# Moving weight splits, gate quotients and query products in a polysketch-attention and expert-mix kernel, with one more expert's block in three passes

## The chip, the cores and the metric

The kernel runs on one core of a Trainium2 chip, in one launch. The metric is the device time in microseconds (us): lower is better. All times below are of runs on the chip.

## The reference

The first half is a polynomial-sketch attention on q, k and v of shape (4, 4, 1088, 32), the second half a mix of four expert networks on the 4352 tokens that come out of it (all in float32):

```python
def phi(x):                       # S1, S2: 8 x 32
    a = einsum('rd,bhsd->bhsr', S1, x); b = einsum('rd,bhsd->bhsr', S2, x)
    return einsum('bhsi,bhsj->bhsij', a, b).reshape(..., 64)
kv, z = einsum('bhsf,bhsd->bhfd', phi(k), v), phi(k).sum(axis=2)
attn = einsum('bhsf,bhfd->bhsd', phi(q), kv) / (einsum('bhsf,bhf->bhs', phi(q), z) + 1e-6)
x = attn.transpose(0, 2, 1, 3).reshape(4352, 128)
p = domain_probs / (domain_probs.sum(-1) + 1e-9)          # 4352 x 4
out = sum over e of p[:, e] * (relu(x @ w1[e]) @ w2[e])     # w1[e]: 128 x 1024, w2[e]: 1024 x 128
```

## The kernel before

**Tiling.** The 4352 tokens go through the experts in 11 chunks: chunk 0 and chunk 10 have 128 tokens, chunks 2 and 3 have 480, the others 448. A chunk takes 16 steps, four for each expert, and a step has two half steps, one for each block of 128 hidden columns (8 blocks for an expert). A half step is called h here, counted over the whole kernel from 0: chunk 1 has h = 32 to 63, chunk 2 has 64 to 95, and so on. The attention of the later batches is cut into units (128, 448 and 512 tokens in the first batch, 576 and 512 in the others), and its pieces are laid between the half steps by lists of half steps.

**First product.** In chunks 1 to 9 a block's hidden values come from three passes of matmuls in the reduced type fp32r, with the tokens and w1 each split into parts: L1158 (`xa`, `wa`) and L1159 (`xb`, `wb`), then ScalarE scales the sum in PSUM (L1160), then L1210 (`xd`, `wd`) adds the third pass. The L1210 of block h is issued behind the L1158 and L1159 of block h+1. Behind it ScalarE makes the rectified part `ha` (L1214), or the plain hidden tile `hid` (L1219).

**Second product.** Six of the eight blocks of an expert (`THREE`: 0, 1, 3, 4, 5, 6) are multiplied by w2 in three fp32r passes (L1283): `ha` by the weight part a, `hb` by b, `hd` by d. VectorE makes `hb` for each block (L1186) and `hd` for two blocks at once (L1189). Blocks 2 and 7 are multiplied in full float32 (`hid`, `w_sb`). For the pairs of chunk and expert in `MORE_IN`, block 2 is done in three passes too. In chunk 1, experts 0 and 1 are done in full float32 for all blocks (L1264). The order of these passes is written out in `DEAL` and `DEAL_MORE` (slots in half steps behind the expert's first).

**The splits of w2.** `second_weight_parts(e)` makes the parts a, b, d of expert e's six blocks in five calls. They work in place: the same columns `a` hold first w2 times 4096, rounded, and later w2 itself, rounded:

```python
split(a[:, first_part], w[:, first_part], 4096.0)                                   # part 1: ScalarE, 256 columns
split(a[:, other_part], w[:, other_part], 4096.0); low(*lows[0])                    # part 2: ScalarE 512, VectorE 256
split(a[:, first_part], w[:, first_part], 1.0);    low(*lows[1])                    # part 3: ScalarE 256, VectorE 512
split(a[:, other_part], w[:, other_part], 1.0)                                      # part 4: ScalarE 512
for c, z, b in lows: join(d[:, c:z], b, 1.0, a[:, c:z], ALU.subtract)               # part 5: VectorE 256 and 512
```

`lows[0]` reads the 256 columns of `first_part`, `lows[1]` the 512 of `other_part`; each `low` reads `w` and `a` and writes `b`. In the profile the splits are L901 (`vab<-w_sb`), the lows L904 (`vab<-w_sb,vab` with 256 columns, `vb<-w_sb,vab` with 512), and part 5 is L904 (`vd`). `W2_AT` names the half step h of each of the five calls; its four tuples are for the experts 2, 3, 0, 1 in this order.

`more_weight_parts(e)` does the same for block 2 alone, in two calls (`vm`; one split and one join of 128 columns each), behind the two steps that `MORE_AT` names. `weight_part` splits w1, `token_parts` splits the tokens of the next chunk (`xa` on ScalarE, `xb` and `xd` on VectorE).

**Order within a half step.** `first` issues L1158, L1159, L1160, then `third` (L1210 and the L1214 or L1219 of the block before), then

```python
lower()     # hb, and hd for a full pair, of the block before
work()      # what the lists lay at this half step: W2_AT, then the attention's plan
```

and then the second products that are due. Calls laid at a step (`MORE_AT`, tokens) come behind its second half step. Every engine works through its own instructions in the order in which they are issued; semaphores that are placed by the operands make it wait for other engines.

**The start.** Chunk 0 (h = 0 to 31, in plain float32) needs unit 0 of the attention alone. Beside it unit 1 (448 tokens) is done by VectorE in `queries`, a generator whose calls are laid at the half steps of `FIRST_AT` (counted from 1): two shuffles and an add (calls 1 to 3), a shuffle and two products (4 to 6), the same again (7 to 9), a split of w1 (10), then from call 13 the attention's matmuls (`kvx,qp`), the division, and copies into the ring of tokens (`ring<-y`, L723, calls 17 and 18). `gate_quotients` (L346 to L352) makes the gates of the two short chunks on VectorE: an add, a reciprocal, two multiplications. It is called behind step 2. The gates are first used at L1247, behind step 5.

Of the kernel before, what the change touches and what calls it, by code (L numbers as in the profile page):

```python
# [24 lines left out]
def kernel(  # L25
# [63 lines left out]
        ("b", 1, 1, 16), ("d", 1, 1, 17), ("b", 2, 0, 16), ("d", 2, 0, 17), ("b", 2, 1, 17), ("d", 2, 1, 18),  # L89
        ("a", 3, 1, 17), ("b", 3, 0, 19), ("b", 3, 1, 19), ("d", 3, 0, 20), ("d", 3, 1, 20),  # L90
    ]
    W2_AT = (36, 37, 38, 39, 40), (40, 41, 42, 43, 44), (45, 46, 47, 47, 49), (54, 57, 60, 63, 66)
    TOKENS_AT = 11, 12

    CHUNKS = [P, 448, 480, 480] + [448] * 6 + [P]
    NC = len(CHUNKS)
    MORE_IN = {(2, 2), (3, 2), (4, 2), (5, 2), (6, 2), (7, 0), (7, 1), (7, 2), (8, 0), (8, 1), (8, 2), (9, 0), (9, 1), (9, 2), (9, 3)}
    MORE_AT = {0: (100, 102), 1: (56, 57), 2: (38, 39), 3: (129, 131)}
    START = [sum(CHUNKS[:m]) for m in range(NC)]
    assert all(sum(u) == S for u in UNITS) and sum(CHUNKS) == B * S  # L100

# [43 lines left out]
    def load_batch(b):  # L145
        load_rows(k, b, "kn")
        vn[b] = load_v(b)
# [32 lines left out]
    def more(m, e):  # L180
        return (m, e) in MORE_IN

# [172 lines left out]
    def gate_rows():  # L355
        nc.vector.reciprocal(dsum[:, :], dsum[:, :])
        nc.gpsimd.tensor_tensor(
            out=_ap(pn, 0, P, 0, [[E, G], [1, E]]), in0=dp[:, :, :], in1=_ap(dsum, 0, P, 0, [[1, G], [0, E]]), op=ALU.mult
        )
# [450 lines left out]
    def add(hs, run):  # L810

        plan.setdefault(hs, []).append(run)

    FIRST_AT = (1, 2, 4, 5, 7, 9, 10, 12, 14, 15, 15, 15, 17, 18, 18, 19, 21, 23, 23)
    KEYS_AT = {
        1: ((36, 37, 38), (38, 39, 40), (39, 40, 41), (48, 48, 52, 65)),
        2: ((79, 79, 79), (83, 84, 85), (84, 85, 86), (90, 93, 97, 100)),
# [8 lines left out]
    def lay_plan():  # L826

        of_first = queries(0, P, UNITS[0][1])
        for at in FIRST_AT:
            add(at, lambda: next(of_first, None))  # L830
# [32 lines left out]
    def queries(b, c, n):  # L863
        qc = early.pop((b, c))
        qf = apool.tile([P, n], F32, tag="qf", name="qf")
        nc.vector.stream_shuffle(in_=qc[:, 0:n], out=qf[:, 0:n], mask=mask_lo)
        yield
        nc.vector.tensor_tensor(out=qf[:, 0:n], in0=qc[:, 0:n], in1=qf[:, 0:n], op=ALU.add)
        yield
        qb = apool.tile([P, QW], F32, tag="qb", name="qb")  # L870
        nc.vector.stream_shuffle(in_=qf[:, 0:n], out=qb[:, 0:n], mask=mask_b)
        yield
        qp = query_tiles()
        for x in range(2):
            qa = apool.tile([P, QW], F32, tag="qa", name="qa")
            nc.vector.stream_shuffle(in_=qf[:, 0:n], out=qa[:, 0:n], mask=mask_a[x])
            yield
            for p in range(2):
                query_product(qp, p, x, n, qa, qb)
                yield  # L880
        weight_part("b", 0, 0)
        yield
        yield
        yield
        yield from attend(b, c, n, qp)
# [20 lines left out]
    def weight_part(what, e, h):  # L906

        c = slice(F // 2 * h, F // 2 * (h + 1))
        w, a, b, d = (x[:, c] for x in (w1_of[e], wa[:, e], wb[:, e], wd[:, e]))
        if what == "a":  # L910
            split(a, w, 4096.0)
        elif what == "b":
            join(b, w, -4096.0, a.bitcast(F32), ALU.add)
        else:
            join(d, a.bitcast(F32), -R12, b.bitcast(F32), ALU.subtract)
# [3 lines left out]
    def second_weight_parts(e):  # L919


        w, n = w2_of[e, 0], N3 * DM
        vab = cpool.tile([P, F], F32R, tag=f"w1_{e}", name="vab")
        vb = cpool.tile([P, 2 * n - F], F32R, tag=f"vb_{e}", name="vb")
        a, lows = vab[:, 0:n], [(0, F - n, vab[:, n:F]), (F - n, n, vb[:, :])]
        first_part, other_part = (slice(c, z) for c, z, _ in lows)

        def low(c, z, b):
            join(b, w[:, c:z], 4096.0, a[:, c:z].bitcast(F32), ALU.subtract)

        split(a[:, first_part], w[:, first_part], 4096.0)
        yield
        split(a[:, other_part], w[:, other_part], 4096.0)
        low(*lows[0])
        yield
        split(a[:, first_part], w[:, first_part], 1.0)
        low(*lows[1])
        yield
        split(a[:, other_part], w[:, other_part], 1.0)
        yield  # L940
        d = cpool.tile([P, n], F32R, tag=f"w2_{e}0", name="vd")[:, :]
        for c, z, b in lows:
            join(d[:, c:z], b.bitcast(F32), 1.0, a[:, c:z].bitcast(F32), ALU.subtract)
        w2_parts[e] = {
            THREE[i]: tuple(
                x[:, DM * i - c : DM * i - c + DM] for x, c in ((a, 0), next((x, c) for c, z, x in lows if DM * i < z), (d, 0))
            )
            for i in range(N3)
        }
        yield  # L950

    def more_weight_parts(e):

        k, w = OTHER[0], second_weight(e, OTHER[0])
        if e % 2 == 0:
            if "sr" not in more_home:
                more_home["sr"] = cpool.tile([P, 6 * P], F32R, tag="sr", name="vm")
            a, b, d = (more_home["sr"][:, P * i : P * i + P] for i in range(3 * (e // 2), 3 * (e // 2) + 3))
        else:
            ab = apool.tile([P, 2 * P], F32R, tag="kvz", bufs=2, name="vm")  # L960
            a, b = ab[:, 0:P], ab[:, P : 2 * P]
            d = (apool if e == 1 else cpool).tile([P, P], F32R, tag="rd" if e == 1 else "sq", name="vm")[:, :]
        split(a, w, 4096.0)
        join(b, w, 4096.0, a.bitcast(F32), ALU.subtract)
        yield
        split(a, w, 1.0)
        join(d, b.bitcast(F32), 1.0, a.bitcast(F32), ALU.subtract)
        w2_parts[e][k] = a, b, d
        yield
# [374 lines left out]
    def at_step(step, *calls):  # L1344
        to_part.setdefault(step, []).extend(calls)

    def next_of(parts_of):
        return lambda: next(parts_of, None)

    for what, e, h, step in SPLITS:  # L1350
        at_step(step, lambda p=(what, e, h): weight_part(*p))
    for e, at in zip((2, 3, 0, 1), W2_AT):
        parts_of = second_weight_parts(e)
        for hs in at:
            at_half.setdefault(hs, []).append(next_of(parts_of))
    for e, at in MORE_AT.items():
        parts_of = more_weight_parts(e)
# [23 lines left out]
    def behind(at):  # L1381

        was = closed[0]
        while due and due[0][0] <= at:
            _, _, _, i, j, what = due.pop(0)
            m, kq = steps[i]
            e, f = divmod(kq, NP)
            if what:
                passed(m, e, what, 2 * f + j, hid[i][j])
                continue  # L1390
            second(i, j)
            if i == NQ - 1:
                unit_project(0)
                unit_rows(0)
            if f == NP - 1 and j == 1:
                close(m, e)
        return closed[0] != was
# [16 lines left out]
    for i in range(len(steps) + LA):  # L1414
        if i < len(steps):
            m, kq = steps[i]
            assert have[0] >= START[m] + CHUNKS[m]

            def work():

                now[0] += 1
                for part in at_half.get(now[0] - 1, ()):
                    part()
                for run in plan.pop(now[0], ()):
                    run()

            first(i, work, lambda j: behind(2 * i + j))
            to_due(i)
            if kq == NQ - 4 and 0 < m < NC - 2:
                assert have[0] >= START[m + 1] + CHUNKS[m + 1]  # L1430
            for part in to_part.get(i, ()):
                part()
            if i == 2:
                gate_quotients()
            elif i == 8:
                later_weights()
            elif i == 5:
                load_batch(1)
            elif i == 24:
                load_batch(2)  # L1440
            elif i == 12:
                gate_rows()
            elif i == 13:
                later_mask()
                store_gates(range(1))
            elif i in (18, 20):
                load_gates(1, [(i - 18) // 2], nc.gpsimd)
            elif 14 <= i < 14 + B - 1:
                store_gates(range(i - 13, i - 12))
            if m == NC - 2 and kq == NQ // 2:  # L1450
                assert have[0] == B * S and not plan
                load_last()
        if i == LA:

            made_hp[3] = psum(ps_h, "h")
            for c in (0, HP):
                half_columns(3, made_hp[3], c)
        if NQ * (NC - 1) <= i < NQ * (NC - 1) + 2:
            continue
        if not behind(2 * i + 1):  # L1460
            next(ending, None)
# [29 lines left out]
```

## Time and profile before

| what | value |
|---|---|
| time, median of 3 runs (lowest to highest) | 446.25 us (445.92 to 446.32) |
| the profiled execution: its own time, its span | 446.1 us, 444.3 us |
| PE busy (TensorE, matmuls) | 438.4 us, 99% of the span |
| PEld busy (TensorE, weight loads) | 370.2 us, 83% |
| DVE busy (VectorE) | 380.1 us, 86% |
| ACT busy (ScalarE) | 335.0 us, 75% |
| POOL busy (GpSimd) | 138.3 us, 31% |
| granted TensorE clock | 1.000 |

The span runs from the first to the last instruction; 1.8 us of the execution's time lie outside it. In the timeline rows that follow, a row has its start and its length in us, the engine, the line of the kernel, the operation, the tiles (written <- read), its shape and how many instructions were merged; a bracket gives the idle time of the engine before it and what ended it. Matmuls are pipelined: a row of 0.36 us may be followed by the next matmul after 0.20 us, so distances between starts are read, not lengths.

### The profile page before, as it was taken

What the parts mean: (1) busy time and instruction counts of PE and PEld (TensorE: products, weight loads), DVE (VectorE), ACT (ScalarE), POOL (GpSimd) and SP (SyncE); (2) the same over time, 40 slices, a digit from 0 to 9 for tenths busy, and PEclk for the clock granted to TensorE, in tenths of its full rate; (3) what the DMA queues carried; (4) which work ended last, traced back from release to release, by engine and by line L of the source; (5) the groups of instructions that cost most, each with busy time, mean ns of one, the idle gap of its engine ahead of it and who ended that gap; (6) DMA issues with size and microseconds to landing.
All of it is one profiled execution on the core that took longest, in us unless ns stands there. A gap on an engine that the chain in (4) does not pass through costs nothing.

```text
span 444.3 us, 8576 instructions
## 1 busy us (share of the span) xinstructions
PE 438.4 (99%) x2988; PEld 370.2 (83%) x2988; DVE 380.1 (86%) x625; ACT 335.0 (75%) x715; POOL 138.3 (31%) x221
## 2 busy tenths in 40 slices
PE   8999999999999999999999999999999999999997
PEld 5887677888877888888888888888888888888886
DVE  5998979978999889889987888899988898898853
ACT  4478889857887588868885888787888888888831
POOL 7349523311143023213321333133423313331430
PEclk9999999999999999999999999999999999999999
DMA  6966266215502340245024601342300020017401
GB/s 192 296 158 169 82 173 119 73 45 129 154 24 45 90 123 22 63 91 142 22 43 72 140 21 31 84 132 53 58 21 21 32 53 22 21 40 208 168 2 28
DMA packets 51155, 38.46 MB, mean 87 GB/s; under 512 B 24968, under 2 KB 45384, under 8 KB 51112
## 3 DMA queue, kind: packets, MB, share of 16 engines
q1 hardware_dynamic: 49672, 36.79, 31.9%
q0 software_dynamic: 1216, 1.06, 1.0%
q8 instruction: 23, 0.38, 0.3%
q14 instruction: 20, 0.16, 0.1%
q10 hardware_dynamic: 224, 0.07, 0.1%
HBM read 32.68 MB, written 5.21 MB: 85 GB/s over the span
## 4 chain that ended last, share of the span: by engine, by line
PE 93%; DVE 2%; ACT 2%; DMA 1%; issue 1%; SPq 0%; DVEq 0%; ACTq 0%
PE o L1283 39%; PE h L1210 13%; PE h L1158 13%; PE h L1159 13%; PE h L262 7%; PE o L1264 3%; PE o L262 3%; PE h L457 1%; DMA kn<-in_k_dram 1%; DVE qp L594 1%; ACT h L1160 0%; DMA vn<-in_v_dram 0%; ACT vab L901 0%; ACT ha L1214 0%; PE h L1128 0%
## 5 line engine op out<-in xcount | busy, mean ns | idle before, releaser
L1160 ACT ACTIVATE h<-h 128x448 f32<-128x448 f32 (+1 forms) x288 | 155.3, 539 | 68.4 <-PE h L1159 64.1
L1186 DVE SCALAR_TENSOR_TENSOR hb<-h,ha 128x448 fp32r<-128x448 f32 (+1 forms) x219 | 134.5, 625 | 30.1 <-ACT ha L1214 26.8
L1189 DVE SCALAR_TENSOR_TENSOR hd<-ha,hb 128x896 fp32r<-128x896 f32 (+3 forms) x117 | 130.2, 1113 | 10.6 <-PE o L1283 0.9
L1158 PE MATMUL h<-xa,wa 128*128 128x448 f32 (+1 forms) x288 | 129.4, 449 | 0.0
L1214 ACT ACTIVATE ha<-h 128x448 fp32r<-128x448 f32 (+1 forms) x219 | 120.0, 548 | 0.0
L1322 POOL TENSOR_TENSOR ev<-ev,gate 128x256 f32<-128x256 f32 (+2 forms) x54 | 48.6, 901 | 215.7 <-DVE ev L1315 207.2
L1210 PE MATMUL h<-xd,wd 128*128 128x448 f32 (+1 forms) x288 | 107.1, 372 | 0.4 <-ACT h L1160 0.3
L1159 PE MATMUL h<-xb,wb 128*128 128x448 f32 (+1 forms) x288 | 106.1, 368 | 0.0
L1283 PE MATMUL o<-ha,vab 128*128 128x448 f32 (+1 forms) x204 | 75.7, 371 | 0.0
L1158 PEld LDWEIGHTS h<-xa,wa 128*128 128x128 f32 x288 | 54.2, 188 | 16.8 <-issue 12.1
L1159 PEld LDWEIGHTS h<-xb,wb 128*128 128x128 f32 x288 | 54.2, 188 | 16.7 <-issue 12.4
L1283 PE MATMUL o<-hd,vd 128*128 128x448 f32 (+1 forms) x204 | 61.6, 372 | 0.0
L1210 PEld LDWEIGHTS h<-xd,wd 128*128 128x128 f32 x288 | 54.0, 188 | 8.9 <-ACT h L1160 2.7
L1283 PE MATMUL o<-hb,vb 128*128 128x448 f32 (+1 forms) x136 | 50.1, 368 | 0.0
L1283 PE MATMUL o<-hid,w_sb 128*128 128x448 f32 (+1 forms) x106 | 49.3, 546 | 0.0
L1324 POOL TENSOR_TENSOR total<-total,ev 128x256 f32<-128x256 f32 (+2 forms) x54 | 46.2, 856 | 4.2
L1283 PEld LDWEIGHTS o<-hd,vd 128*128 128x128 f32 x204 | 37.9, 188 | 4.5 <-issue 0.8
L1283 PEld LDWEIGHTS o<-ha,vab 128*128 128x128 f32 x204 | 38.3, 188 | 3.8
L1219 ACT ACTIVATE hid<-h 128x448 f32<-128x448 f32 (+1 forms) x69 | 38.0, 551 | 1.0 <-PE h L1210 0.8
L1322 POOL TENSOR_TENSOR total<-ev,gate 128x256 f32<-128x256 f32 (+2 forms) x18 | 12.3, 707 | 57.0 <-issue 39.6
L1283 PEld LDWEIGHTS o<-hb,vb 128*128 128x128 f32 x136 | 25.5, 188 | 2.3
L1283 PE MATMUL o<-hb,vab 128*128 128x448 f32 (+1 forms) x68 | 25.1, 368 | 0.0
(157 smaller groups left out, 463.2 us busy)
## 6 DMA issues: line engine op xcount, KB each, us to landing
gate<-gates SPq DMA_DIRECT2D x22, 224.0 KB, 3.3
kn<-in_k_dram SPq DMA_DIRECT2D x4, 544.0 KB, 6.9
vn<-in_v_dram SPq DMA_DIRECT2D x16, 128.0 KB, 4.5
qp<-qd SPq DMA_DIRECT2D x8, 256.0 KB, 3.4
w_last<-in_moe_w_dram SPq DMA_DIRECT2D x4, 512.0 KB, 5.0
qp<-qd SPq DMA_DIRECT2D x6, 288.0 KB, 4.8
qb<-qd SPq DMA_DIRECT2D x6, 288.0 KB
w_sb<-in_moe_w_dram SPq DMA_DIRECT2D x3, 512.0 KB
```

Of the source, the lines that this page charges most:

```text
L262: nc.tensor.matmul(out(s), weights(s), moving(s), **flags)
L1158: nc.tensor.matmul(g, wa[:, e, w], xa, start=True, stop=False)
L1159: nc.tensor.matmul(g, wb[:, e, w], xb, start=False, stop=True)
L1160: nc.scalar.activation(g, g, ACTF.Copy, scale=1.0 + R12)
L1186: nc.vector.scalar_tensor_tensor(out=hb, in0=g, scalar=0.0, in1=high, op0=ALU.max, op1=ALU.subtract)
L1189: nc.vector.scalar_tensor_tensor(out=d2, in0=a2.bitcast(F32), scalar=R12, in1=b2.bitcast(F32), op0=ALU.mult, op1=ALU.subtract)
L1210: nc.tensor.matmul(g, w, x, start=False, stop=True, skip_group_check=True)
L1214: nc.scalar.activation(ha, g, ACTF.Relu, scale=NEAR)
L1219: nc.scalar.activation(hid[i][j], g, ACTF.Relu)
L1283: nc.tensor.matmul(acc[m, e][o][:, 0:n], w, h, start=first_one, stop=last)
L1322: nc.gpsimd.tensor_tensor(out=to[:, x], in0=ev[:, x], in1=g[:, x], op=ALU.mult)
L1324: nc.gpsimd.tensor_tensor(out=total[m][:, x], in0=total[m][:, x], in1=ev[:, x], op=ALU.add)
```

## The change

Five lists or conditions get other values; no instruction is written anew.

- `W2_AT`: the five parts of expert 0's split move from h = 45, 46, 47, 47, 49 to 45, 46, 50, 51, 52, those of expert 1 from 54, 57, 60, 63, 66 to 52, 53, 54, 60, 63. Experts 2 and 3 keep theirs.
- `MORE_IN` gets the pair (5, 0): in chunk 5, block 2 of expert 0 is multiplied in three passes.
- `MORE_AT`: block 2 of expert 0 is split behind steps 61 and 62 and no longer behind 100 and 102, that of expert 3 behind 77 and 78 and no longer behind 129 and 131.
- `FIRST_AT`: calls 3 to 9 of `queries` come at half steps 3 to 9 and no longer at 4, 5, 7, 9, 10, 12, 14. The later calls stay.
- `gate_quotients` is called behind step 4, not behind step 2.

```diff
-    W2_AT = (36, 37, 38, 39, 40), (40, 41, 42, 43, 44), (45, 46, 47, 47, 49), (54, 57, 60, 63, 66)
+    W2_AT = (36, 37, 38, 39, 40), (40, 41, 42, 43, 44), (45, 46, 50, 51, 52), (52, 53, 54, 60, 63)
...
-    MORE_IN = {(2, 2), (3, 2), (4, 2), (5, 2), (6, 2), (7, 0), (7, 1), (7, 2), (8, 0), (8, 1), (8, 2), (9, 0), (9, 1), (9, 2), (9, 3)}
-    MORE_AT = {0: (100, 102), 1: (56, 57), 2: (38, 39), 3: (129, 131)}
+    MORE_IN = {(2, 2), (3, 2), (4, 2), (5, 0), (5, 2), (6, 2), (7, 0), (7, 1), (7, 2), (8, 0), (8, 1), (8, 2), (9, 0), (9, 1), (9, 2), (9, 3)}
+    MORE_AT = {0: (61, 62), 1: (56, 57), 2: (38, 39), 3: (77, 78)}
...
-    FIRST_AT = (1, 2, 4, 5, 7, 9, 10, 12, 14, 15, 15, 15, 17, 18, 18, 19, 21, 23, 23)
+    FIRST_AT = (1, 2, 3, 4, 5, 6, 7, 8, 9, 15, 15, 15, 17, 18, 18, 19, 21, 23, 23)
...
-            if i == 2:
+            if i == 4:
                 gate_quotients()
```

## The prediction

> **What bounds the kernel.** I read the page first: engine sums and the chain that ended last.
>
> ```profile
> PE 438.4 (99%) x2988; PEld 370.2 (83%) x2988; DVE 380.1 (86%) x625; ACT 335.0 (75%) x715; POOL 138.3 (31%) x221
> PE 93%; DVE 2%; ACT 2%; DMA 1%; issue 1%; SPq 0%; DVEq 0%; ACTq 0%
> ```
>
> TensorE is the path: only matmuls taken away, stalls removed and new waits count. So I looked in TensorE's timeline for distances above the usual 0.20 us.
>
> ```profile
> 20.46 0.64 PE L262 MATMUL h<-kvx,qp 128*64 128x66 f32 x16
> 21.30 0.69 PE L262 MATMUL h<-kvx,qp 128*64 128x66 f32 x16 [0.21 <-DVE qp L594]
> ...
> 55.56 0.37 PE L1159 MATMUL h<-xb,wb 128*128 128x448 f32 x1
> 56.00 0.47 PE L1210 MATMUL h<-xd,wd 128*128 128x448 f32 x1
> 56.31 0.54 PE L1264 MATMUL o<-hid,w_sb 128*128 128x448 f32 x1
> ...
> 68.32 0.37 PE L1159 MATMUL h<-xb,wb 128*128 128x448 f32 x1
> 68.96 0.47 PE L1210 MATMUL h<-xd,wd 128*128 128x448 f32 x1 [0.27 <-ACT h L1160]
> ```
>
> Four stalls lie where the change works. At 20.87 the unit's matmuls wait 0.38 for the last query product and lose 0.05 more on restarting: 0.43. At 55.56 the distance is 0.44 for 0.20, and the next 0.31 for 0.20: a stall and its restart, 0.34 (0.10 of it the restart, which I add to each new stall too). At 68.32 it is 0.44 + 0.10 = 0.54, at 76.72 0.13 + 0.10 = 0.23. From 80 us on I find none above 0.07. The last three wait for ScalarE's L1160, which stands behind splits of w2:
>
> ```profile
> 54.16 0.54 ACT L1219 ACTIVATE hid<-h 128x448 f32<-128x448 f32 x1
> 54.58 0.94 ACT L901 ACTIVATE vab<-w_sb 128x256 fp32r<-128x256 f32 x2
> 55.41 0.54 ACT L1160 ACTIVATE h<-h 128x448 f32<-128x448 f32 x1
> ```
>
> That pair is parts 3 and 4 of expert 0, at h = 47; expert 1's 512-column splits stand at 67.35 and 75.92. Then VectorE, which makes the other half of each split, and GpSimd beside it:
>
> ```profile
> 58.21 0.68 DVE L904 SCALAR_TENSOR_TENSOR vd<-vb,vab 128x512 fp32r<-128x512 f32 x1
> 58.81 0.62 DVE L1186 SCALAR_TENSOR_TENSOR hb<-h,ha 128x448 fp32r<-128x448 f32 x1
> 59.47 1.09 DVE L1189 SCALAR_TENSOR_TENSOR hd<-ha,hb 128x896 fp32r<-128x896 f32 x1
> 60.48 0.62 DVE L1312 COPY ev<-o 128x448 f32<-128x448 f32 x1
> 61.47 0.62 DVE L1186 SCALAR_TENSOR_TENSOR hb<-h,ha 128x448 fp32r<-128x448 f32 x1 [0.38 <-ACT ha L1214]
> 62.90 0.63 DVE L1186 SCALAR_TENSOR_TENSOR hb<-h,ha 128x448 fp32r<-128x448 f32 x1 [0.80 <-ACT ha L1214]
> 63.56 1.34 DVE L1189 SCALAR_TENSOR_TENSOR hd<-ha,hb 128x896 fp32r<-128x896 f32 x1
> ```
>
> It runs 1 to 2 us behind TensorE in h = 49 to 54, just where the parts go.
>
> **First chunk (query products, quotients): 0.05 us lost.** VectorE works without a gap from 14.46 to 25.99, when its last `ring` copy ends. Today the order is shuffle (to 17.05), quotients, products, with L1247 (20.26) ahead of the last product (20.63 to 21.25). In the new order the quotients (17.05 to 17.60, 0.55) and L1247 (0.36) follow the products; the last product ends near 20.35, ahead of 20.92, and the stall of 0.43 goes. But the same work still precedes the ring copies, so these end where they did, or 0.06 later. ScalarE's `xa` waits for them (26.11, with 0.27 idle), the rectification of step 12 stands behind it and ends at 26.96, and the weight load that needs it starts at 27.01, with no reserve. TensorE, 0.43 earlier, waits 0.43 there. With a late copy and a restart the net is 0 to 0.15 lost; I take 0.05. The quotients are off the path: L1247 comes near 21.0, and its PSUM bank is wanted at 23.57.
>
> **Expert 0 in three passes in chunk 5: 0.16 gained.** A float32 block costs 0.75 (62.04 to 62.99 less one pass), three passes 0.61. Stage lengths agree: chunk 6's expert 0 takes 10.05, chunk 7's, with three passes, 9.69, and a plain stage behind such a one 10.25 for 10.05: -0.36 + 0.20. VectorE gains one L1186 (0.54 with the overlap of 0.08) and half an L1189 (0.6): 1.15 in a stage (216.62 to 226.66) that has 1.82 idle; without that cover up to 0.16 is lost again.
>
> **Splits of block 2 at steps 61, 62 and 77, 78: nothing.** Each call is a split of 0.31 on ScalarE and a join of 0.28 on VectorE. ScalarE idles 0.28, 0.43, 0.20 and 0.57 ahead of the L1160 behind them; VectorE has gaps of 0.24 to 0.27, and the closest consumer (L1283 with `hd`, 178.04) has 0.83 in hand. Without that cover, 0.3 each. No moved piece issues a DMA or a GpSimd instruction, so no queue of transfers is touched.
>
> **The splits of experts 0 and 1.** Gains first. Without the pair at 54.58, L1160 starts at 54.61 and the stall of 0.34 goes. Without expert 1's splits at 67.35 and 75.92, 0.54 and 0.23 go: L1160 then ends near 68.39, for an L1210 wanted at 68.52.
>
> Against them stand two waits that the trace of before does not have. Part 4 overwrites the 512 columns that VectorE's `lows[1]` of part 3 reads; part 3 overwrites the 256 that `lows[0]` of part 2 reads. So ScalarE may not start the split before VectorE has done the join, and L1160 of that half step stands behind the split. Before, a join was done in time (53.74 to 54.39, split at 54.58). Now the joins lie at h = 50 and 53 and the splits one half step later, and the join comes behind `hb` and `hd` of the block before (`lower()` precedes `work()`). I walk the queues with the durations above, 0.34 earlier than before; an engine starts 0.03 to 0.05 behind what it waits for, and takes the next ready instruction 0.08 (VectorE) or 0.09 (ScalarE) before the last ends.
>
> First wait. `ha` of block 1 ends at 58.65 - 0.34 = 58.31; `hb` 58.34 to 58.96; `hd` to 60.08; `lows[1]` (0.69, as `vb` elsewhere) 60.00 to 60.69; the split (0.63) 60.72 to 61.35; L1160 (0.53) 61.26 to 61.79; L1210 at 61.84, not at 61.63 - 0.34 = 61.29. That is 0.55, with a restart 0.65; `ha` of block 3 then ends at 62.24 for an L1283 ready at 62.14: 0.15 and a restart more. Together 0.9.
>
> Second wait. `hb` 62.27 to 62.89; expert 0's part 5, 62.81 to 63.83; the next `hb` to 64.37; `hd` 64.40 to 65.49; `lows[0]` (0.42) to 65.83; split (0.42) 65.86 to 66.28; L1160 66.19 to 66.72; L1210 at 66.77, not at 65.23 - 0.34 + 0.9 = 65.79. With a restart 1.08. Part 5 falls beside GpSimd's four gate operations, which follow `ev`:
>
> ```profile
> 62.67 0.60 POOL L1322 TENSOR_TENSOR ev<-ev,gate 128x192 f32<-128x192 f32 x1
> 63.35 0.60 POOL L1324 TENSOR_TENSOR total<-total,ev 128x192 f32<-128x192 f32 x1
> ```
>
> The `hd` that started at 63.56 beside the last took 1.34 for 1.09; at 48.35 and 49.22 the two `vd` took 0.95 and 1.08 for 0.42 and 0.68 beside GpSimd. So part 5 is longer by 0 to 0.93; I take 0.5, near two losses of 0.25. Second wait: 1.08 to 2.0, taken 1.58.
>
> The Trainium skill ("SBUF — State Buffer", Who interferes with whom) says that a VectorE instruction with two SBUF inputs and a GpSimd one that reads SBUF exclude each other for a whole instruction. By that rule part 5 could lose both 0.60, and the sum would come to 448.1; the rows of 1.34 and 0.95 show a loss of that kind, but of a part.
>
> While TensorE waits nobody else gains; h = 60 (part 4, 0.63 for 0.42) fits ScalarE's gap, and at 63 part 5 leaves `hb` of the next chunk over 1 us in hand. Behind 85 us there is no stall that a later TensorE could hide, so the loss stays.
>
> **Sum.** +0.05 - 0.16 - 0.34 + 0.9 + 1.58 - 0.54 - 0.23 = +1.26. Against the profiled execution's 446.1 (span 444.3 and 1.8 around it; the median of the runs is 0.15 above): 447.4. Ends: with no contention and no first-chunk loss +0.7, 446.8; with 2.0 and 0.15, +1.8, 447.9.
>
> **Rivals.** *Faster: no split waits.* If VectorE has both joins done when ScalarE is ready, only gains stay: +0.05 - 0.16 - 0.34 - 0.54 - 0.23 = -1.2, 444.9. It decides at 59.5 for the first join (I have 60.69) and near 64.9 for the second (65.8 to 66.3): they must come about 1.2 us sooner than I place them. For it: ScalarE then fits every split without a delay. Against it: `hb` and `hd` cannot start before `ha`, and no row shows them shorter. Chance 0.14.
>
> *About equal: only one wait counts.* With the second gone: 0.05 - 0.16 - 0.34 + 0.9 - 0.54 - 0.23 = -0.3, 445.8; with the first gone and 1.08 for the second, about 445.9. For it: the second join is reached by the longest walk, and each of its steps could be 0.2 shorter. Chance 0.14.
>
> *Slower than I say:* part 5 loses all of 0.93 and `hb` and `hd` behind it reach their matmuls late, one more stall of 0.3 to 0.6: 448.2 to 448.5. Chance 0.08.
>
> *The edit does not do what it says:* moved query products leave the stall at 20.87, if the last ends after 20.92. That changes nothing, since the wait at 27 hides it; it is part of the forecast.
>
> **Numbers.** The forecast has 0.64 with 446.7 to 448.0 as its own range. The range 445.5 to 448.4 takes in the middle rival and most of the upper one. Steps of 0.2% (0.89 us, about what a measurement of this kernel can tell from no change) from 446.25 lie at 445.36 and 447.14: faster 0.15; slower 0.57 (0.49 of the forecast's 0.64 and the upper rival); the same 0.28.
>
> **What would show it.** Right: a row of ScalarE idle ahead of `vab` that VectorE ends, near 60 and 65 us; L1210 with 0.5 to 0.6 lost near 61.8 and 1 to 1.5 near 67; no stall near 56; TensorE's wait for `qp` gone and one of 0.4 near 27; chunk 5's expert 0 with 9.69. Wrong: `vab` splits with no idle ahead of them, or joins that start before the `hd` issued ahead of them.

## The result and the profile after

The changed kernel takes 448.48 us (median of 6 runs, 448.37 to 448.75) against 446.25 us (445.92 to 446.32): a ratio of 1.0054, interval 1.0043 to 1.0064, slower by 2.2 us. The profiled execution took 448.75 us, its span is 447.0 us.

The page's engine sums and the chain that ended last:

```profile
PE 439.5 (98%) x2989; PEld 370.4 (83%) x2989; DVE 382.8 (86%) x627; ACT 335.4 (75%) x715; POOL 139.2 (31%) x221
PE 91%; DMA 3%; DVE 3%; ACT 1%; SPq 1%; issue 1%; POOL 0%; ACTq 0%; DVEq 0%
```

TensorE's work is the same but for one block, and its share of the chain falls from 93% to 91%. Where the time went is seen in TensorE's timeline at the places that the prediction named:

```profile
20.70 1.10 PE L262 MATMUL h<-kvx,qp 128*64 128x66 f32 x32
...
27.73 0.66 PE L262 MATMUL o<-w_sb,hid 128*64 128x128 f32 x8 [0.68 <-ACT hid L1136]
...
62.58 0.47 PE L1210 MATMUL h<-xd,wd 128*128 128x448 f32 x1 [0.40 <-ACT h L1160]
63.04 0.47 PE L1283 MATMUL o<-ha,vab 128*128 128x448 f32 x1
...
68.41 0.47 PE L1210 MATMUL h<-xd,wd 128*128 128x448 f32 x1 [1.69 <-ACT h L1160]
```

The unit's query matmuls, two rows with a stall between them before, are now one row of 32. TensorE waits at 27.73 instead, and at 62.58, 63.04 and 68.41, where it did not wait before. ScalarE's timeline has the reason for the last three:

```profile
61.46 0.63 ACT L901 ACTIVATE vab<-w_sb 128x512 fp32r<-128x512 f32 x1 [1.05 <-DVE vb L904]
62.00 0.53 ACT L1160 ACTIVATE h<-h 128x448 f32<-128x448 f32 x1
...
67.50 0.42 ACT L901 ACTIVATE vab<-w_sb 128x256 fp32r<-128x256 f32 x1 [1.81 <-DVE vab L904]
67.83 0.53 ACT L1160 ACTIVATE h<-h 128x448 f32<-128x448 f32 x1
```

Each split stands idle until VectorE ends a `low`, and the L1160 that L1210 needs stands behind it. VectorE's timeline on the way to the second wait, and GpSimd's beside it:

```profile
63.56 0.84 DVE L904 SCALAR_TENSOR_TENSOR vd<-vab 128x256 fp32r<-128x256 f32 x1
64.33 1.09 DVE L904 SCALAR_TENSOR_TENSOR vd<-vb,vab 128x512 fp32r<-128x512 f32 x1
65.34 0.61 DVE L1186 SCALAR_TENSOR_TENSOR hb<-h,ha 128x448 fp32r<-128x448 f32 x1
65.98 1.09 DVE L1189 SCALAR_TENSOR_TENSOR hd<-ha,hb 128x896 fp32r<-128x896 f32 x1
67.00 0.42 DVE L904 SCALAR_TENSOR_TENSOR vab<-w_sb,vab 128x256 fp32r<-128x256 f32 x1
```

```profile
63.53 0.60 POOL L1322 TENSOR_TENSOR ev<-ev,gate 128x192 f32<-128x192 f32 x1
64.21 0.66 POOL L1324 TENSOR_TENSOR total<-total,ev 128x192 f32<-128x192 f32 x1
```

Part 5 (`vd`) took 0.84 and 1.09 where 0.42 and 0.68 are its lengths alone: 0.83 lost beside GpSimd. The first found 0.57 of GpSimd's operation still to run (63.53 + 0.60 - 63.56), the second 0.54.

In the first chunk VectorE's L1247, which starts at 20.26 in before with no idle time ahead of it, now stands behind a gap:

```profile
20.26 0.35 DVE L1247 TENSOR_SCALAR end<-o,ends 128x128 f32<-128x128 f32 x1
```

```profile
21.07 0.36 DVE L351 TENSOR_SCALAR ends<-ends,e_sum 128x4 f32<-128x4 f32 x2
21.84 0.35 DVE L1247 TENSOR_SCALAR end<-o,ends 128x128 f32<-128x128 f32 x1 [0.41 <-PE h L262]
```

Executions differ by up to 0.5 us in when chunk 0 begins (13.43 to 13.96), so I compare distances between starts of L1158: before's in the first row, differences from it below, for this kernel and e1 to e10, which are explained in the next section. "First chunk" is from chunk 0's first matmul to h = 32; the last column goes to the last half step. The stretches left out differ by at most 0.04 each.

| kernel | first chunk | h 48–57 | 57–60 | 60–78 | 128–160 (chunk 4) | 160–168 | 168–176 | all |
|---|---|---|---|---|---|---|---|---|
| before | 14.76 | 12.22 | 4.20 | 24.35 | 42.56 | 10.04 | 14.43 | 408.87 |
| the change | +0.47 | +2.52 | -0.52 | -0.21 | +0.20 | -0.33 | +0.28 | +2.40 |
| e1 splits alone | +0.01 | +2.51 | -0.51 | -0.19 | +0.02 | +0.01 | -0.02 | +1.85 |
| e2 first chunk alone | +0.44 | 0 | 0 | +0.01 | 0 | +0.01 | -0.02 | +0.44 |
| e3 three passes alone | 0 | 0 | -0.01 | +0.01 | +0.21 | -0.35 | +0.30 | +0.19 |
| e4 products only | -0.06 | 0 | 0 | +0.04 | 0 | 0 | 0 | -0.01 |
| e5 expert 0's parts | +0.01 | +0.59 | 0 | +0.01 | +0.04 | +0.02 | -0.01 | +0.70 |
| e6 part 5 later | 0 | +1.40 | -0.52 | -0.21 | +0.01 | +0.01 | -0.02 | +0.72 |
| e7 design | +0.01 | -0.37 | -0.38 | -0.23 | +0.01 | +0.01 | -0.02 | -0.99 |
| e8 quotients at step 3 | +0.08 | 0 | 0 | +0.01 | 0 | +0.02 | -0.01 | +0.11 |
| e9 expert 1's parts | +0.01 | +1.06 | -0.53 | -0.20 | 0 | 0 | 0 | +0.37 |
| e10 early block-2 splits | +0.01 | 0 | 0 | +0.03 | +0.02 | -0.33 | +0.43 | +0.20 |

The prediction's terms for these columns were +0.05; -0.34 + 0.9 + 1.58 = +2.14; -0.54; -0.23; 0; -0.36 and +0.20. Three are off by 0.2 or more, all to the slow side: the first chunk, h 48–57 and chunk 4.

### The profile page after: what moved, and what is told of

Read it like the earlier page. It is cut to its first block, busy times and chain, and to the rows that moved or that the text cites. A ratio compares the mean times of both kernels' runs of the same rounds, so it can differ in the third digit from the quotient of the medians.

```text
span 447.0 us, 8576 instructions
## 1 busy us (share of the span) xinstructions
PE 439.5 (98%) x2989; PEld 370.4 (83%) x2989; DVE 382.8 (86%) x627; ACT 335.4 (75%) x715; POOL 139.2 (31%) x221
## 3 DMA queue, kind: packets, MB, share of 16 engines
q0 software_dynamic: 1216, 1.06, 0.9%
## 4 chain that ended last, share of the span: by engine, by line
PE 91%; DMA 3%; DVE 3%; ACT 1%; SPq 1%; issue 1%; POOL 0%; ACTq 0%; DVEq 0%
PE o L1283 39%; PE h L1210 13%; PE h L1158 13%; PE h L1159 13%; PE h L262 6%; PE o L1264 2%; DMA w_sb<-in_moe_w_dram 2%; PE o L262 2%; PE h L457 1%; SPq L172 1%; DMA dp<-in_moe_domain_probs_dram 1%; DVE hb L1186 0%; DVE vd L904 0%; DVE hd L1189 0%; DVE ring L723 0%
## 5 line engine op out<-in xcount | busy, mean ns | idle before, releaser
L1160 ACT ACTIVATE h<-h 128x448 f32<-128x448 f32 (+1 forms) x288 | 155.2, 539 | 66.8 <-PE h L1159 60.4
L1189 DVE SCALAR_TENSOR_TENSOR hd<-ha,hb 128x896 fp32r<-128x896 f32 (+3 forms) x118 | 129.7, 1099 | 10.7 <-PE o L1283 0.9
L1158 PE MATMUL h<-xa,wa 128*128 128x448 f32 (+1 forms) x288 | 129.1, 448 | 0.0
L1210 PE MATMUL h<-xd,wd 128*128 128x448 f32 (+1 forms) x288 | 107.0, 371 | 2.2 <-ACT h L1160 2.1
L1158 PEld LDWEIGHTS h<-xa,wa 128*128 128x128 f32 x288 | 54.2, 188 | 16.7 <-issue 11.9
L1210 PEld LDWEIGHTS h<-xd,wd 128*128 128x128 f32 x288 | 54.0, 188 | 10.5 <-ACT h L1160 3.9
L1324 POOL TENSOR_TENSOR total<-total,ev 128x256 f32<-128x256 f32 (+2 forms) x54 | 47.8, 885 | 4.2
```

Source lines behind the costliest of these rows:

```text
L1158: nc.tensor.matmul(g, wa[:, e, w], xa, start=True, stop=False)
L1160: nc.scalar.activation(g, g, ACTF.Copy, scale=1.0 + R12)
L1189: nc.vector.scalar_tensor_tensor(out=d2, in0=a2.bitcast(F32), scalar=R12, in1=b2.bitcast(F32), op0=ALU.mult, op1=ALU.subtract)
L1210: nc.tensor.matmul(g, w, x, start=False, stop=True, skip_group_check=True)
L1324: nc.gpsimd.tensor_tensor(out=total[m][:, x], in0=total[m][:, x], in1=ev[:, x], op=ALU.add)
```

## The experiments

All but e13 to e15 (3 rounds) were timed in 5 rounds against before on the same chip; a difference in us is that of the two medians. All edits are on the kernel before.

### The change in its three parts

**e1**, the splits alone:

```diff
-    W2_AT = (36, 37, 38, 39, 40), (40, 41, 42, 43, 44), (45, 46, 47, 47, 49), (54, 57, 60, 63, 66)
+    W2_AT = (36, 37, 38, 39, 40), (40, 41, 42, 43, 44), (45, 46, 50, 51, 52), (52, 53, 54, 60, 63)
```

> Only the new half steps of the splits of experts 0 and 1; everything else as before. My theory (two split waits that the old places did not have): the prediction's terms -0.34 + 0.9 + 1.58 - 0.54 - 0.23 give +1.4 us; the trace of the whole change reads +1.76 for the same five places, so +1.4 to +1.8 over 446.25. Rival 'one wait counts': -0.3 to +0.3. Rival 'faster': -1.1. If it is +1.8, the rest of the change (+0.4 to +0.5) has to show in the other two parts.

Measured 448.02 against 446.03: +1.99, ratio 1.0044 (1.0031 to 1.0056); by the table +1.85. The two waits are there and most of the loss with them; the rivals in which one or none of them counts are out.

**e2**, the query products and the quotients:

```diff
-    FIRST_AT = (1, 2, 4, 5, 7, 9, 10, 12, 14, 15, 15, 15, 17, 18, 18, 19, 21, 23, 23)
+    FIRST_AT = (1, 2, 3, 4, 5, 6, 7, 8, 9, 15, 15, 15, 17, 18, 18, 19, 21, 23, 23)
...
-            if i == 2:
+            if i == 4:
                 gate_quotients()
```

> Only the query products at half steps 3 to 9 and the gate quotients behind step 4. The prediction had +0.05 (0 to 0.15). The trace of the whole change shows VectorE idle for 0.41 us ahead of L1247 and half step 32 starting 0.72 later, of which 0.24 was there before any changed instruction. If that gap comes from the new order, +0.4 to +0.5 and the gap is there again; if it was a chance of one execution, +0.0 to +0.1 and no gap.

Measured 446.44 against 446.03: +0.41, ratio 1.0009 (1.0000 to 1.0018); by the table +0.44. The gap of VectorE is there again (0.38, its rows are shown with e14): it belongs to the new order, not to one execution.

**e3**, (5, 0) in `MORE_IN` and the moved splits of block 2:

```diff
-    MORE_AT = {0: (100, 102), 1: (56, 57), 2: (38, 39), 3: (129, 131)}
+    MORE_AT = {0: (61, 62), 1: (56, 57), 2: (38, 39), 3: (77, 78)}
```

> Only expert 0 of chunk 5 with block 2 in three passes, and the splits of block 2 of experts 0 and 3 at steps 61, 62, 77, 78. The prediction had -0.16 (three passes -0.36, the stage behind +0.20, moved splits 0). The stage lengths of the whole change read -0.33 in chunk 5's expert 0, +0.28 in its expert 1 and +0.16 in chunk 4: +0.1. So -0.16 if the prediction's term holds, +0.1 if the trace's does.

Measured 446.27 against 446.03: +0.24; the interval (0.9995 to 1.0012) holds 1, but the places in the table are those of the whole change, +0.21, -0.35 and +0.30. VectorE's and TensorE's weight-load timelines of e3 show why:

```profile
174.20 0.76 DVE L904 SCALAR_TENSOR_TENSOR vm<-vm 128x128 fp32r<-128x128 f32 x1
...
176.87 1.16 DVE L1189 SCALAR_TENSOR_TENSOR hd<-ha,hb 128x960 fp32r<-128x960 f32 x1
...
184.14 1.23 DVE L801 TENSOR_TENSOR qp<-qp,qb 128x576 f32<-128x576 f32 x1
...
191.03 0.61 DVE L1315 TENSOR_TENSOR ev<-ev,o 128x448 f32<-128x448 f32 x1
```

```profile
191.70 0.30 PEld L1283 LDWEIGHTS o<-hid,w_sb 128*128 128x128 f32 x2 [0.22 <-DVE ev L1315]
...
234.10 0.30 PEld L1283 LDWEIGHTS o<-hid,w_sb 128*128 128x128 f32 x2 [0.26 <-DVE ev L1315]
```

The block-2 join (`vm`) takes 0.76 for 0.28 beside GpSimd's `total`. `hd` starts at 176.87, 0.71 later than before when its start-up offset of 0.10 is taken off, and the matmul that reads it has no reserve left (0.05 lost). VectorE catches up in part (0.49 idle ahead of 182.47), but then L801 meets GpSimd (1.23 for 0.74; in before it was the `hd` ahead of it, 1.37 for 1.09), and at 191.03 `ev`, which frees the bank `o`, is still 0.25 late: the first `hid`,`w_sb` matmul of the next expert waits, 0.12 lost. In chunk 5 (234.10) the added `hb` and `hd` do the same: 0.14 lost. Together with e1 and e2 the three parts give 1.99 + 0.41 + 0.24 = 2.64 by medians, 2.48 by the table, for 2.40 of the whole: they add up.

### The two split waits

**e5**, only expert 0's tuple new:

```diff
-    W2_AT = (36, 37, 38, 39, 40), (40, 41, 42, 43, 44), (45, 46, 47, 47, 49), (54, 57, 60, 63, 66)
+    W2_AT = (36, 37, 38, 39, 40), (40, 41, 42, 43, 44), (45, 46, 50, 51, 52), (54, 57, 60, 63, 66)
```

> Only expert 0's five parts at the new half steps (45, 46, 50, 51, 52); expert 1's stay at 54, 57, 60, 63, 66. My theory: the pair at h = 47 goes (-0.34) and the first split wait comes (+0.9): +0.5 to +0.6 by the replay of the queues, with the stalls at 68.32 and 76.72 still there and no second wait, although part 5 meets GpSimd as in the whole change. Rival 'part 5 beside GpSimd costs by itself': over +1.2.

Measured 446.68 against 446.15: +0.53, ratio 1.0012 (1.0003 to 1.0021); h 48–57 is longer by 0.59 = -0.34 + 0.93. Part 5 took 0.84 and 1.08 here too, and h = 56, where the second wait would be, is 0.01 longer: nobody waits behind it.

**e9**, only expert 1's tuple new:

```diff
-    W2_AT = (36, 37, 38, 39, 40), (40, 41, 42, 43, 44), (45, 46, 47, 47, 49), (54, 57, 60, 63, 66)
+    W2_AT = (36, 37, 38, 39, 40), (40, 41, 42, 43, 44), (45, 46, 47, 47, 49), (52, 53, 54, 60, 63)
```

> Only expert 1's five parts at the new half steps (52, 53, 54, 60, 63); expert 0's stay at 45, 46, 47, 47, 49. If the two waits were independent, this is the rest of the whole: 1.99 - 0.53 = +1.46. My theory is that most of the second wait is expert 0's part 5 ahead of expert 1's first join; with part 5 back at h = 49 the replay of the queues gives a second wait of 0.98 less 0.58 and 0.23: +0.2.

Measured 446.34 against 446.11: +0.23, ratio 1.0003 (0.9995 to 1.0012); by the table +1.06 for the wait, -0.53 and -0.20 for the stalls. The second wait is 1.92 in the whole change and 1.06 here, so about 0.9 us belong to the meeting of the two tuples; the table's totals give 0.8 (1.85 less 0.70 and 0.37), the medians 1.2 (1.99 less 0.53 and 0.23). That most of the wait is part 5, as expected, does not follow from this run: more than half of it is there with part 5 back at h = 49. Of the 1.06, 0.25 is an `hd` beside GpSimd (63.29, 1.34 for 1.09).

**e6**, both tuples new, but expert 0's part 5 at h = 56:

```diff
-    W2_AT = (36, 37, 38, 39, 40), (40, 41, 42, 43, 44), (45, 46, 47, 47, 49), (54, 57, 60, 63, 66)
+    W2_AT = (36, 37, 38, 39, 40), (40, 41, 42, 43, 44), (45, 46, 50, 51, 56), (52, 53, 54, 60, 63)
```

> The new half steps of both experts, but expert 0's part 5 at h = 56 and not at 52, so that it no longer stands ahead of expert 1's first join on VectorE and no longer meets GpSimd's four gate operations there. My theory: the second wait falls from 1.92 to about 1.0; by the replay of the queues the whole is +0.8 over before without a loss to GpSimd at its new place and +1.2 with one, against +1.8 to +2.0 with part 5 at 52. Rival 'the second wait does not hang on part 5': +1.8 again.

Measured 446.74 against 446.15: +0.59, ratio 1.0012 (1.0004 to 1.0021). The second wait is 1.40 - 0.59 = 0.81. VectorE's and ScalarE's timelines of e6:

```profile
64.04 1.09 DVE L1189 SCALAR_TENSOR_TENSOR hd<-ha,hb 128x896 fp32r<-128x896 f32 x1
65.05 0.42 DVE L904 SCALAR_TENSOR_TENSOR vab<-w_sb,vab 128x256 fp32r<-128x256 f32 x1
...
68.64 0.42 DVE L904 SCALAR_TENSOR_TENSOR vd<-vab 128x256 fp32r<-128x256 f32 x1
68.98 0.68 DVE L904 SCALAR_TENSOR_TENSOR vd<-vb,vab 128x512 fp32r<-128x512 f32 x1
```

```profile
65.56 0.42 ACT L901 ACTIVATE vab<-w_sb 128x256 fp32r<-128x256 f32 x1 [0.70 <-DVE vab L904]
```

With part 5 out of the way the split waits 0.70 and not 1.81, and part 5 has its own lengths, away from GpSimd. One number of the tuple was worth 1.1 us by the second wait and by the table (1.85 less 0.72); the medians give 1.4.

**e7**, half steps chosen by replaying the queues so that each split comes after the join whose input it overwrites:

```diff
-    W2_AT = (36, 37, 38, 39, 40), (40, 41, 42, 43, 44), (45, 46, 47, 47, 49), (54, 57, 60, 63, 66)
+    W2_AT = (36, 37, 38, 39, 40), (40, 41, 42, 43, 44), (45, 46, 47, 48, 49), (50, 52, 55, 60, 63)
```

> Only other half steps for the splits, chosen so that each split comes after the join that it waits for: expert 0 at 45, 46, 47, 48, 49 (part 4 alone one half step later than before), expert 1 at 50, 52, 55, 60, 63. My theory: the stalls at 55.56, 68.32 and 76.72 go (-0.34, -0.54, -0.23) and no split waits: -1.1 (-0.8 where part 5 loses to GpSimd). Rival 'the stalls come back elsewhere': 0 to -0.3.

Measured 445.22 against 446.15: -0.93, ratio 0.9977 (0.9968 to 0.9987). The view of waits between 54 and 80 us (us in total, times, longest), first of before, then of the changed kernel, then of e7:

```profile
PEld h L1210 <- ACT h L1160: 2.1, 5, 0.7
PE h L1210 <- ACT h L1160: 0.3, 1, 0.3
```

```profile
PEld h L1210 <- ACT h L1160: 3.3, 3, 2.1
PE h L1210 <- ACT h L1160: 2.1, 2, 1.7
ACT vab L901 <- DVE vab L904: 1.8, 1, 1.8
ACT vab L901 <- DVE vb L904: 1.1, 1, 1.1
```

```profile
PEld h L1210 <- ACT h L1160: 0.8, 3, 0.4
```

No split waits in e7, and of L1210's waits 0.8 is left. Half step by half step the three stalls of before give back 0.33, 0.47 and 0.24; a new loss of 0.11 at h = 57 takes a part of it.

### VectorE's gap in the first chunk

**e4**, `FIRST_AT` new, the quotients behind step 2 as before:

```diff
-    FIRST_AT = (1, 2, 4, 5, 7, 9, 10, 12, 14, 15, 15, 15, 17, 18, 18, 19, 21, 23, 23)
+    FIRST_AT = (1, 2, 3, 4, 5, 6, 7, 8, 9, 15, 15, 15, 17, 18, 18, 19, 21, 23, 23)
```

> Only the query products at half steps 3 to 9; the gate quotients stay behind step 2, between the shuffle and the first products. VectorE then has the quotients at 16.95 as before, products to about 20.6, and L1247 behind them. If the gap ahead of L1247 hangs on the quotients being the instructions just ahead of it, there is no gap here and the time is 0 to +0.1; if it hangs on the products (or the query matmuls behind them), it is here too and the time +0.4.

Measured 445.97 against 446.03: -0.06, ratio 0.9998 (0.9989 to 1.0007). No gap. The stall at 20.87 shrinks here and does not go (0.22 of 0.43 is left, as the last product ends only 0.2 earlier), and about as much as was gained is lost again near 27.

**e8**, e4 with the quotients behind step 3, so that a product lies between them and L1247:

```diff
-            if i == 2:
+            if i == 3:
                 gate_quotients()
```

> Early query products, and the gate quotients behind step 3: one product lies between the quotients and L1247, which still waits for the quotients and for TensorE. If VectorE's gap of 0.38 to 0.41 ahead of L1247 comes only where the quotients stand directly ahead of it, no gap and -0.1 to +0.1; if it comes from L1247's second wait as such, the gap is there and +0.4.

Measured 446.25 against 446.15: +0.10, ratio 1.0003 (0.9994 to 1.0011), no gap. The last product now ends late again, and 0.35 of the stall at 20.87 is left.

**e13**, in e2 the split of w1 at half step 11:

```diff
-    FIRST_AT = (1, 2, 4, 5, 7, 9, 10, 12, 14, 15, 15, 15, 17, 18, 18, 19, 21, 23, 23)
+    FIRST_AT = (1, 2, 3, 4, 5, 6, 7, 8, 9, 11, 15, 15, 17, 18, 18, 19, 21, 23, 23)
```

> The first-chunk part alone, with the split of w1 (VectorE, 0.68) laid at half step 11 and not at 15, so that it stands between the gate quotients and L1247. If the gap of 0.4 needs L1247 directly behind the quotients, it is gone and the time is -0.1 to +0.1; if L1247's own waits make it, the gap stays and +0.4.

Measured 446.29 against 446.07: +0.22, ratio 1.0004 (0.9994 to 1.0013). VectorE is idle 0.16 ahead of the split and not at all ahead of L1247; the first chunk is 0.25 longer than before. The split does not wait for the quotients, and the profile shows no releaser for this idle time; it starts 0.51 behind a wait instruction of its own (20.614).

**e14**, in e2 a small copy behind the quotients (it moves the lines below it by one):

```diff
+        nc.vector.tensor_copy(out=e_sum[:, :, 0], in_=e_sum[:, :, 1])
```

> The first-chunk part alone, with one more small VectorE copy (two elements a partition, into a column that nobody reads later) between the quotients and L1247. If any instruction between them takes the gap away, +0.1; if the gap is a time that must pass between the quotients and L1247 (0.4 from the end of the first), the gap is 0.2 to 0.3 and the time +0.4.

Measured 446.37 against 446.07: +0.30, ratio 1.0006 (0.9996 to 1.0015); first chunk +0.19, of which about 0.1 is the added copy.

**e15**, in e2 the two last quotient instructions swapped:

```diff
-        for i in range(2):
+        for i in (1, 0):
```

> The first-chunk part alone, with the two last quotient instructions in the other order, so that L1247 reads what the instruction directly ahead of it has written (in the other order it was written one instruction earlier). If the gap comes from a wait that is met while the second one still runs, it shrinks to under 0.1 and the time is +0.0 to +0.1; if it is there whatever the order, +0.4.

Measured 446.77 against 446.07: +0.70, ratio 1.0020 (1.0010 to 1.0029); first chunk +0.61. VectorE's timelines of e2, e14 and e15 in this order:

```profile
20.72 0.36 DVE L351 TENSOR_SCALAR ends<-ends,e_sum 128x4 f32<-128x4 f32 x2
21.46 0.35 DVE L1247 TENSOR_SCALAR end<-o,ends 128x128 f32<-128x128 f32 x1 [0.38 <-PE h L262]
```

```profile
20.87 0.36 DVE L351 TENSOR_SCALAR ends<-ends,e_sum 128x4 f32<-128x4 f32 x2
21.14 0.16 DVE L354 COPY e_sum<-e_sum 128x2 f32<-128x2 f32 x1
21.36 0.35 DVE L1248 TENSOR_SCALAR end<-o,ends 128x128 f32<-128x128 f32 x1
```

```profile
21.00 0.36 DVE L351 TENSOR_SCALAR ends<-ends,e_sum 128x4 f32<-128x4 f32 x2
21.90 0.35 DVE L1247 TENSOR_SCALAR end<-o,ends 128x128 f32<-128x128 f32 x1 [0.54 <-PE h L262]
```

With the copy between them L1248 starts 0.13 behind the end of the quotients, so it is not a time that must pass. The profile's releaser is no cause either: L1247 needs expert 0's `o`, whose last matmuls end at 18.69 in the changed kernel's timeline, and in e2 it starts 0.01 ahead of the last semaphore of the query matmuls (21.476). What does fit: the wait for VectorE's own quotients is a separate instruction of the queue (at 20.985 in e2, 21.338 in the changed kernel, 21.396 in e15), and L1247 starts 0.48, 0.51 and 0.51 behind it. In e14, where that wait was met while the copy ran, it is 0.08. So in these runs the gap comes where the wait for the quotients is met with no instruction of work between. It is not bound to L1247 alone, as the split in e13 shows; why it is 0.5 here, where the same kind of wait ahead of L1189 takes 0.07, stays open.

### Three passes with other splits, and the best version

**e10**, (5, 0) in `MORE_IN`, with expert 0's block 2 split early:

```diff
-    MORE_AT = {0: (100, 102), 1: (56, 57), 2: (38, 39), 3: (129, 131)}
+    MORE_AT = {0: (54, 55), 1: (56, 57), 2: (38, 39), 3: (129, 131)}
```

> Expert 0 of chunk 5 in three passes, with block 2 of expert 0 split behind steps 54 and 55 (where ScalarE idles 4.64 us and VectorE 1.16) and that of expert 3 where it was (129, 131). The run with steps 61, 62, 77, 78 gave +0.24 (trace +0.20: 0.17 in chunk 4, -0.35 and +0.30 in chunk 5's experts 0 and 1). My theory: the 0.17 comes from the joins at 61 and 62 that leave VectorE late for half a chunk, and goes: -0.05. If the 0.17 belongs to expert 3's splits or to the longer code, +0.2 again.

Measured 446.15 against 446.11: +0.04, ratio 0.9998 (0.9990 to 1.0007). Chunk 4's 0.2 is gone. This run also has expert 3's splits at their old steps, but in e3 0.18 of the 0.21 is lost by h = 142, ahead of step 77 (h = 154); so it did come from the joins behind steps 61 and 62. The stage behind is +0.43 and not +0.30: `ev` is late there again and TensorE waits 0.38 for it (PEld row at 234.03). -0.33 + 0.43 leaves +0.10: the block in three passes gains nothing here, since VectorE, who does the added work, comes too late with `ev`.

**e11**, the edits of e7 and e4 together:

> The splits of the experts 0 and 1 as in the design without waits (45, 46, 47, 48, 49 and 50, 52, 55, 60, 63) and the query products early, gate quotients behind step 2. Sum of the two single runs: -0.93 - 0.06 = -1.0.

Measured 445.12 against 446.11: -0.99, ratio 0.9976 (0.9966 to 0.9986).

**e12**, the edits of e11 and e10 together:

> The same, with expert 0 of chunk 5 in three passes and its block 2 split behind steps 54 and 55. By my theory -1.0 - 0.05 = -1.05; if three passes cost again, -0.8.

Measured 445.21 against 446.11: -0.90, ratio 0.9982 (0.9973 to 0.9990). No better than e11. The version that beats both kernels is e7 with or without e4; no run separates those two.

## Why the prediction was wrong by 1.1 us

The direction and the main mechanism held: slower, by two split waits that the old half steps did not have. Its signs were there: ScalarE idle ahead of `vab`, L1210 late at both places, no stall near 56, TensorE's wait moved from 20.87 to 27. The misses are three, 0.42 in the first chunk, 0.34 in the second wait and 0.31 in the three passes with their moved splits. The time lies next to the 448.2 to 448.5 of the rival "slower than I say" (its own terms add up to 448.1 to 448.4), but by chance: that rival's further stall behind part 5 did not come, as h 57–60 and 60–78 gained what was forecast. The terms, from the change's row of the table (the halves of h 48–57 from the half steps h = 49, 53 and 56):

- **The pair at h = 47: -0.34**, measured -0.33. **The stalls at 68.32 and 76.72: -0.54 and -0.23**, measured -0.52 and -0.21.
- **First wait: +0.9**, measured +0.92 (+0.93 in e5).
- **Second wait: +1.58, mis-sized; measured 1.92.** The walk held: 1.92 less the 0.83 is 1.09, for 1.08 without contention. The value taken for part 5 beside GpSimd, 0.5 ("near two losses of 0.25"), was the step that failed: it was 0.83, of a bound of 0.93. A loss is not a fixed 0.25. In the rows it is what GpSimd's operation has still to run when VectorE's instruction starts, less about 0.14: `hd` at 63.56 found 0.39 and lost 0.25, part 5 found 0.57 and 0.54 and lost 0.42 and 0.41. Two rows of before had the higher price (`vd` at 48.35 and 49.22, which lost 0.53 and 0.40); I took the lower. The rule of the Trainium skill that I weighed ("SBUF — State Buffer", Who interferes with whom) is exclusion for a whole instruction. The traces are close to it: the later one loses nearly all that is left of the earlier one's operation.
- **First chunk: +0.05, mis-sized; measured +0.41 to +0.47.** The step "the same work still precedes the ring copies, so these end where they did" left out that an order can make VectorE idle. Without the idle time the first chunk costs +0.19 with e14's added copy in it, close to the walk; e4 (-0.06) and e8 (+0.08) come out near the term too, but by another way, as part of the stall at 20.87 stays. Why VectorE idles stays open.
- **Three passes: -0.16, and the moved block-2 splits: nothing; together measured +0.15 to +0.24.** The stage itself gave -0.33 for -0.36 and the one behind it the +0.20. What failed is the cover: "1.82 idle" in the stage, and "0.83 in hand" for `hd`. VectorE's idle time lay in other places than the added work, each join could be lengthened beside GpSimd (0.28 to 0.76), and the late `ev` holds a PSUM bank that TensorE wants. The prediction named the price without cover for chunk 5 (0.16), not for the bank.

Corrected terms: 0.47 - 0.33 + 0.92 + 1.92 - 0.52 - 0.21 + 0.20 - 0.33 + 0.28 = 2.40, the table's total.

## What to carry to other kernels

Work that overwrites in place is not free to move: a split that waits for a join on another engine holds up everything queued behind it, so place it by the time at which the join ends, and keep other work of the joining engine (here part 5) out of the way; one such number was worth 1.1 us. An engine's idle time in a stage is cover only if it comes before the next thing that somebody waits for, including a last reader that frees a bank. Where two engines disturb each other, take the price from what the earlier one has still to run, not from the gentlest row.

## What the runs showed of the hardware

- A VectorE instruction with two inputs from SBUF and a GpSimd operation lengthen each other, and the one that starts later pays. It lost what was left of the other's operation less 0.10 to 0.15, in all of before's rows with more than 0.15 left and at part 5: `hd` 1.34 for 1.09, `vd` 0.84 and 1.09 for 0.42 and 0.68, in e3 `vm` 0.76 for 0.28 and L801 1.23 for 0.74, each with 0.61 left. Part 5 alone, at h = 56, took 0.42 and 0.68. `hb`, which reads `h` from PSUM, lost nothing (61.47 in before, 0.62 with 0.44 left). In e7 `hd` starts first, and GpSimd pays, 1.36 for 0.60:

```profile
63.33 1.09 DVE L1189 SCALAR_TENSOR_TENSOR hd<-ha,hb 128x896 fp32r<-128x896 f32 x1
```

```profile
63.51 1.36 POOL L1324 TENSOR_TENSOR total<-total,ev 128x192 f32<-128x192 f32 x1
```

- VectorE stood idle for 0.38 to 0.54 us between an instruction and the next that waits for VectorE's own result (e2, e15, the changed kernel); with one instruction of 0.16 between them it was under 0.1 (e14).
